# TensorE in source order from the end of the opening, eight slots for each attention unit

## The chip, the cores and the metric

The kernel runs on one core of one Trainium2 chip. The metric is the device time of one execution, in microseconds (us), as the median of several runs. A traced execution of the kernel is read beside it: it has a span, from the first to the last instruction, and a device time of its own.

## The reference

Sliding-window attention with ALiBi biases is followed by a SwiGLU block. There are 8 batches, 8 heads, 576 positions and 64 columns for each head; a query sees itself and the 127 positions before it. The attention output, 4608 tokens by 512 columns, goes through gate and value products to 1536 columns and back to 512. Cut to what matters:

```python
rel = pos[:, None] - pos[None, :]
mask = (rel >= 0) & (rel < 128)
scores = np.where(mask, scale * q @ k.T + slope_h * -abs(rel), -1e9)
attn = softmax(scores)                     # along the keys
x = (attn @ v) -> (4608, 512)
g, val = x @ w_gate, x @ w_val             # (4608, 1536)
out = (g * sigmoid(g) * val) @ w_out       # (4608, 512)
```

## The kernel before

**Attention.** Two batches make a group of 1152 tokens, cut into nine tiles of 128 (eight whole ones, and one that holds the last 64 positions of both batches). There are four groups, so 36 ranks (token tiles) and 36 attention units, numbered i = 0 to 35. A unit's work is in four steps:

- `scores(i)` gives a list of steps: the products of keys and queries on TensorE (tile `ps`, or `psc` for the units at a batch's end), their exponentials on ACT (`ex`, `exc`), and the masks' products on DVE. Unit 9s + p reads k rank 9s + p and q ranks 9s + p and 9s + p + 1.
- `weighted(i)` multiplies with the values (tile `av`) on TensorE and divides by the sums on DVE (tile `x`).
- `x_transposed(i)` brings `x` into the layout of the FFN (tile `xT`): through TensorE (tile `px`) and a copy by ACT for units up to 23, by DMA transposes on SP from 24 on.
- `load(r)` fetches k, q and v of rank r by GpSimd's (POOL's) DMAs, which cast to fp16; `transpose(n)` brings k and q into the layout for scores: on TensorE (tile `pt`) for ranks up to 10, by DMA transposes on SP from rank 11 on. The natural tiles `kn` and `qn` have five buffers each, the transposed ones 12 and 9, the values 12.

**FFN.** Nine blocks of 512 tokens. `gate_val(n, m)` computes 128 columns of gate and value (tiles `pg` and `pv`, four matmuls of 512 columns each), with a tanh on ACT (`tt`) and two products on DVE (`uu`, `hT`). The projection to 512 columns is `project` for block 0 (tile `po`, twelve matmuls of 512 columns for each 128 tokens) and a scheme of seven products on halves, `strassen`, for later blocks. From block 6 on gate and value use seven products too. Block n needs the units whose tokens it holds; `ready` lists how many.

**The order.** `everything` runs the opening, `first_tiles`, written out by hand (units 0 to 3 and the first products of block 0), and then the generator `ffn`, which yields the size of each step it has emitted (1 for a gate or value product, 0.75 for a part of a projection). After each step a target says how many slots of the generator `attention` should have been emitted, and as many are drawn. A slot is what stands between two yields: a step of `scores`, a `weighted`, and so on. `ready` and `blk` are a floor below the target.

What the source says isn't the order on the engines everywhere. Under `tc.manual_schedule` the named engines keep the source's order; elsewhere a scheduler orders the instructions by a simulation of its own. Before, TensorE, DVE and ACT are by hand up to step `ALONE` = 8; then all of them are scheduled; from step `FIXED_FROM` = 60 on TensorE keeps the source's order again. POOL's loads are by hand throughout. SP's queue (transposes and output stores) is scheduled.

In the part of the code that changes, `LATE` = 13 parts two forms of a unit: before it `weighted(i)` follows all of `scores(i + 1)`; from it on `weighted(i)` stands after the third step of `scores(i + 1)`, and `x_transposed` is put off by one unit.

Of the kernel before, what the change touches and what calls it, by code (L numbers as in the profile page):

```python
# [19 lines left out]
X_DMA_FROM = 24  # L20
MASKS_AT = 18.0
ALONE = 8
# [6 lines left out]
FIRST = 4  # L29
LEAD = 6  # L30
PRE = 0
SEVEN_FROM = 6
SILU_AT = 7
SECOND = 5.5
RATE = 54.0
FIXED_FROM = 60
LATE = 13


def slot(h):  # L40

    return 4 * (h // 4) + 2 * (h % 2) + (h % 4) // 2
# [9 lines left out]
def kernel(  # L52
# [95 lines left out]
    def busy(n):  # L148

        t_ = ps_f.tile([P, 512], FP32, name="nil", tag="po", bufs=1)  # L150
        for _ in range(n):
            nc.tensor.matmul(t_, idle[:, 0:P], idle, start=True, stop=True)
# [12 lines left out]
    last = len(units) - 1  # L165
# [28 lines left out]
    def load(rank):  # L194
        load_qk(rank)
        load_v(rank)
# [34 lines left out]
    need = [18 * s + n for s in range(NSUP) for n in (3, 5, 7, 8, 11, 13, 15, 18 if s else 16, 18)]  # L231
# [11 lines left out]
    def scores(i):  # L243

        s, p = units[i]
        def combined(n):
            return scores_128(s, (3, 7, 8)[n], 8, (s, "c", n), msk[n])

        def together(one, two):
            return [one[0] + two[0]] + one[1:] + two[1:]  # L250

        if p == 8:
            first = combined(0) if s == 0 else []
            return first + together(combined(1), combined(2))
        if p == 7 and s == 0:
            return scores_128(s, p, p, (s, p), reg[:, :, 0:P])
        if p == 7:
            return together(scores_128(s, p, p, (s, p), reg[:, :, 0:P]), combined(0))
        if p == 3:
            return scores_128(s, p, p, (s, p), reg[:, :, 0:P], i < FIRST)  # L260
        ks = (9 * s + p) % NK
        banks = []
        early_tile = i < FIRST
        e = epool.tile([P, H, 256], FP16, name="ex", tag="ex", bufs=4)
        ex[(s, p)] = e

        def products():
            for q4 in range(2):
                two = [ps_a.tile([P, 2, 256], FP32, name="ps", tag="a") for _ in range(2)]
                banks.append(two)  # L270
                for par in range(2 if early_tile else 0):
                    o = 4 * q4 + 2 * par
                    nc.tensor.matmul(two[par], idm, bias[:, o:o + 2, :], start=True, stop=False)
                for j in range(2):
                    pair = 2 * q4 + j
                    for par in range(2):
                        rows = slice(64 * par, 64 * par + 64)
                        nc.tensor.matmul(two[par][:, j, :], kT[rows, ks, pair, :],  # L278
                                         qT[rows, p:p + 2, pair, :], start=(j == 0 and not early_tile),
                                         stop=(j == 1))  # L280

        def act(q4, par):
            o = 4 * q4 + 2 * par
            nc.scalar.activation(e[:, o:o + 2, :], banks[q4][par], AF.Exp, scale=scale)  # L284

        def mul(q4):
            if early_tile:
                return
            o = slice(4 * q4, 4 * q4 + 4)
            nc.vector.tensor_mul(e[:, o, :], e[:, o, :], reg[:, o, :])  # L290

        return [[products], [lambda: act(0, 0)], [lambda: act(0, 1), lambda: mul(0)],
                [lambda: act(1, 0)], [lambda: act(1, 1), lambda: mul(1)]]
# [31 lines left out]
    def weighted(i):  # L325

        s, p = units[i]
        x = xpool.tile([P, H, D], FP16, name="x", tag="x")
        xs[i] = x
        for half in range(2):  # L330
            pool, tag = (ps_f, "gv") if i < FIRST else (ps_a, "a")
            av = pool.tile([P, 4, D + 1], FP32, name="av", tag=tag)
            todo = []
            for j in range(4):
                h = 4 * half + j
                if p == 8:
                    for n, kt in enumerate((3, 7, 8)):
                        todo.append((j, ex[(s, "c", n)][:, slot(h), :], va[9 * s + kt][:, h, :]))
                else:
                    if p not in (0, 4):  # L340
                        todo.append((j, ex[(s, p - 1)][:, slot(h), 128:256],
                                     va[9 * s + p - 1][:, h, :]))
                    todo.append((j, ex[(s, p)][:, slot(h), 0:128], va[9 * s + p][:, h, :]))
            for n, (j, w, val) in enumerate(todo):
                nc.tensor.matmul(av[:, j, :], w, val, start=(n == 0), stop=(n == len(todo) - 1))  # L345
            rec = xpool.tile([P, 4, 1], FP32, name="rec", tag="rec", bufs=4)
            nc.vector.reciprocal(rec, av[:, :, D:D + 1])
            nc.vector.tensor_mul(x[:, 4 * half:4 * half + 4, :], av[:, :, 0:D],  # L348
                                 rec.broadcast_to([P, 4, D]))
# [429 lines left out]
    def loads_to(r):  # L779
        nonlocal loaded  # L780
        while loaded <= min(r, NR - 1):
            load(loaded)
            loaded += 1

    def transposes_to(n):
        nonlocal done_t
        while done_t < n:
            transpose(done_t)
            done_t += 1

    def ahead(i):

        n = need[min(i + 4, last)]
        while done_t < n and order[done_t][1] < loaded and order[done_t][1] >= QK_DMA_FROM:
            transposes_to(done_t + 1)

    def run(steps):
        for fs in steps:
            for f in fs:
                f()  # L800
            yield
# [34 lines left out]

    def attention():

        waiting = []
        transposes_to(need[FIRST])  # L840
        for _ in run(scores(FIRST)):
            yield FIRST
        for i in range(FIRST, last + 1):
            late = i >= LATE
            if i < last:
                transposes_to(need[i + 1])
                for n, _ in enumerate(run(scores(i + 1))):
                    yield i - len(waiting)
                    if n == 2 and late:
                        weighted(i)  # L850
                        yield i - len(waiting)
            if not late or i == last:
                weighted(i)
                yield i
            loads_to(i + 7)
            ahead(i)
            yield i - len(waiting)
            if late and i < X_DMA_FROM:
                if waiting:
                    x_transposed(waiting.pop(0))  # L860
                waiting.append(i)
                yield i
                yield i
                continue
            while waiting:
                x_transposed(waiting.pop(0))
            x_transposed(i)
            yield i
            yield i + 1

    def load_w(c0, c1):
        for src, dst in ((wg2, wg_sb), (wv2, wv_sb)):
# [62 lines left out]

    def everything():
        nonlocal done
        base = 0
        busy(WARM)
        with tc.manual_schedule(engines=ENGINES[MANUAL]):  # L940
            first_tiles()
            done = FIRST
            steps = progress(ffn())
            while (at := next(steps)) < ALONE:
                if at == 2.0:
                    nc.scalar.copy(idm2, idm)
                if at in (1.0, 3.0, 4.0):
                    later_masks(2 * (1, 3, 4).index(at) + 2, 2)
        fixed = ExitStack()
        for step in steps:  # L950
            if step >= FIXED_FROM and fixed is not None:
                fixed.enter_context(tc.manual_schedule(engines=ENGINES["pe"]))
                fixed, held = None, fixed
            if step == MASKS_AT:
                make_masks()

            b1 = 24 + 3 * PRE

            lead = LEAD if done < X_DMA_FROM - 2 else LEAD + 4
            blk = (0 if step + LEAD < b1 else 1 if step + LEAD < 60  # L960
                   else min(NBLK - 1, 2 + int((step + lead - 60) // 34.5)))
            if step < b1:

                target = base + 1.25 * max(0, step - ALONE) + 1.5 * max(0, step - 16)
            elif step < 60:
                target = base + 32 + SECOND * 8 * (step - b1) / (60 - b1)
            else:
                target = 84 + (step - 57) * RATE / 34.5
            while (n_att < target or done < ready[blk]) and att_step():
                pass  # L970
        held.close()

    everything()
    queue.close()

# [29 lines left out]
```

## Time and profile before

| | us |
|---|---|
| median of 3 runs (345.45, 346.0, 348.52) | 346.0 |
| profiled execution, its own time | 347.1 |
| its span | 345.3 |
| TensorE (PE) busy | 329.6 (95%) |
| DVE busy | 277.8 (80%) |
| ACT busy | 207.6 (60%) |
| POOL busy | 109.6 (32%) |

The profiled execution is one run of the program with the hardware profiler on. Busy times are unions of an engine's instructions; an engine can be idle because it waits for data, for a free buffer, or because it has nothing to do. A line of a timeline reads: start, length, engine, source line, operation, tile written, tile read, shapes, count, and in brackets how long the engine sat idle before it and what ended that. `PEld` is the loading of weights, which runs beside the matmuls; `POOLq` and `SPq` are DMA issues. DMA load lines show only the issue; the time to landing is a separate figure. Line numbers are those of the kernel before.

### The profile page before, as it was taken

Reading aid. Unit: us, or ns where it says so; the run is one execution under the profiler, and the core shown is the slowest. Engines: PE = TensorE matmul, PEld = TensorE weight load, DVE = VectorE, ACT = ScalarE, POOL = GpSimd, SP = SyncE. Lnnn points to the kernel's source line nnn. Section 1 sums busy time; section 2 is a strip of 40 time slices with the busy share of each in tenths; the row PEclk is TensorE's granted clock in tenths of the full one; section 3 lists DMA queues with packets and bytes.
Section 4 is the critical chain, followed back from the end, with each engine's and each line's share of the span. In section 5 each row is a group of like instructions: output and inputs, shape, how many; then the busy total and the mean of one; then the engine's idle time right before and its main releaser. Section 6 shows DMA issues by size and latency. Waiting matters only on the chain.

```text
span 345.3 us, 7777 instructions
## 1 busy us (share of the span) xinstructions
PE 329.6 (95%) x2983; PEld 218.6 (63%) x2983; DVE 277.8 (80%) x652; ACT 207.6 (60%) x412; POOL 109.6 (32%) x136
## 2 busy tenths in 40 slices
PE   7999987999999999999999999999999999999995
PEld 4484444444456655565565565566788878888884
DVE  6578884999888769998899999999855875775683
ACT  3758675555675666666565646563467676776640
POOL 8967690748665166825008000000000000000000
PEclk9999999999999999999999999999999999999999
DMA  9999999999999999999959904021101101011014
GB/s 152 170 180 175 158 165 154 96 119 157 137 174 138 154 177 161 168 164 135 205 115 103 173 18 93 15 63 47 63 2 61 61 1 64 2 62 63 0 70 116
DMA packets 160037, 37.37 MB, mean 108 GB/s; under 512 B 147328, under 2 KB 155648, under 8 KB 160000
## 3 DMA queue, kind: packets, MB, share of 16 engines
q0 software_dynamic: 118336, 18.62, 85.3%
q1 hardware_dynamic: 40976, 17.64, 27.0%
q10 hardware_dynamic: 688, 0.62, 0.6%
q8 instruction: 23, 0.38, 0.5%
q14 instruction: 14, 0.11, 0.1%
HBM read 37.91 MB, written 9.44 MB: 137 GB/s over the span
## 4 chain that ended last, share of the span: by engine, by line
PE 66%; DVE 17%; DMA 7%; ACT 4%; issue 3%; POOL 2%; SPq 0%; DVEq 0%; ACTq 0%; POOLq 0%
PE po L532 14%; PE pv L397 12%; PE pg L397 12%; PE gX L623 8%; PE gY L623 4%; PE av L345 3%; DMA wo_sb<-in_moe_w_out_dram 3%; DVE uu L416 3%; DMA va<-in_v_dram 3%; PE p L532 2%; DVE hT L427 2%; PE ps L278 2%; PE gZ L623 2%; PE po L451 2%; DVE x L348 2%
## 5 line engine op out<-in xcount | busy, mean ns | idle before, releaser
L397 PE MATMUL pv<-xT,wv_sb 128*128 128x512 f16 (+2 forms) x320 | 76.5, 358 | 0.6 <-DVE uu L416 0.3
L397 PE MATMUL pg<-xT,wg_sb 128*128 128x512 f16 (+2 forms) x320 | 75.8, 358 | 0.3 <-DVE xT L373 0.2
L415 ACT ACTIVATE tt<-pg 128x512 f16<-128x512 f32 (+2 forms) x70 | 41.3, 590 | 50.5 <-PE pg L397 49.5
L284 ACT ACTIVATE ex<-ps 128x512 f16<-128x512 f32 x96 | 50.0, 606 | 11.6 <-PE ps L278 11.6
L416 DVE SCALAR_TENSOR_TENSOR uu<-tt,pg 128x512 f16<-128x512 f16 (+2 forms) x69 | 45.9, 666 | 10.4 <-ACT tt L415 10.2
L427 DVE TENSOR_TENSOR hT<-uu,pv 128x512 f16<-128x512 f16 (+2 forms) x70 | 46.6, 666 | 3.3 <-PE pv L397 1.6
L185 POOL DMA_DIRECT2D va<-in_v_dram x40 | 34.3, 867 | 37.3 <-PE av L345 31.7
L397 PEld LDWEIGHTS <-wg_sb 128*128 128x128 f16 x320 | 28.2, 98 | 24.4 <-issue 2.2
L397 PEld LDWEIGHTS <-wv_sb 128*128 128x128 f16 x320 | 28.3, 98 | 24.1 <-issue 3.0
L532 PEld LDWEIGHTS <-hT 128*128 128x128 f16 x384 | 36.8, 98 | 10.4 <-issue 1.1
L191 POOL DMA_DIRECT2D kn<-in_k_dram x39 | 33.3, 858 | 24.9 <-DMA kT<-kn 13.4
L191 POOL DMA_DIRECT2D qn<-in_q_dram x39 | 33.4, 863 | 13.9 <-DMA va<-in_v_dram 8.0
L532 PEld LDWEIGHTS <-S 128*128 128x128 f16 x288 | 27.6, 98 | 10.7 <-issue 2.5
L290 DVE TENSOR_TENSOR ex<-ex,m_reg 128x1024 f16<-128x1024 f16 x42 | 28.7, 687 | 3.2 <-ACT ex L284 3.1
L348 DVE TENSOR_TENSOR x<-av,rec 128x256 f16<-128x256 f32 x72 | 28.5, 419 | 0.4
L532 PE MATMUL po<-T,S 128*128 128x256 f16 x192 | 26.5, 273 | 0.5 <-DVE S L487 0.5
L532 PE MATMUL po<-T,hT 128*128 128x256 f16 x192 | 26.0, 273 | 0.0
L317 ACT ACTIVATE exc<-psc 128x512 f16<-128x512 f32 x40 | 21.3, 608 | 4.1 <-PE psc L313 4.1
L675 DVE TENSOR_TENSOR hT<-s,v 128x512 f16<-128x512 f16 x18 | 7.6, 423 | 18.5 <-ACT s L674 18.5
L345 PEld LDWEIGHTS <-ex 128*128 128x128 f16 x384 | 17.4, 97 | 4.6 <-issue 1.2
L345 PE MATMUL av<-va,ex 128*128 128x65 f16 x384 | 19.3, 193 | 0.7 <-ACT ex L284 0.7
L278 PE MATMUL ps<-qT,kT 64*128 64x256 f16 x192 | 16.6, 272 | 0.4 <-DVE qT L223 0.2
(134 smaller groups left out, 536.6 us busy)
## 6 DMA issues: line engine op xcount, KB each, us to landing
out_dram<-osb SPq DMA_DIRECT2D x32, 256.0 KB, 2.5
va<-in_v_dram POOLq DMA_DIRECT2D x32, 128.0 KB, 9.0
qn<-in_q_dram POOLq DMA_DIRECT2D x31, 128.0 KB, 7.9
kn<-in_k_dram POOLq DMA_DIRECT2D x31, 128.0 KB, 8.3
wg_sb<-in_moe_w_gate_dram POOLq DMA_DIRECT2D x6, 256.0 KB, 7.7
wv_sb<-in_moe_w_val_dram POOLq DMA_DIRECT2D x6, 256.0 KB, 8.3
wo_sb<-in_moe_w_out_dram POOLq DMA_DIRECT2D x2, 768.0 KB, 9.6
kn<-in_k_dram POOLq DMA_DIRECT2D x8, 64.0 KB, 6.9
```

What stands on the lines that cost most here:

```text
L185: nc.gpsimd.dma_start(va[rank][p0:p1, :, 0:D], src)
L191: nc.gpsimd.dma_start(t_[p0:p1], src)
L284: nc.scalar.activation(e[:, o:o + 2, :], banks[q4][par], AF.Exp, scale=scale)
L290: nc.vector.tensor_mul(e[:, o, :], e[:, o, :], reg[:, o, :])
L345: nc.tensor.matmul(av[:, j, :], w, val, start=(n == 0), stop=(n == len(todo) - 1))
L348: nc.vector.tensor_mul(x[:, 4 * half:4 * half + 4, :], av[:, :, 0:D], rec.broadcast_to([P, 4, D]))
L397: nc.tensor.matmul(ps[:, c0:c1], w[:, kb, ms], xT[n][:, kb, c0:c1], start=(kb == 0 and c0 == 0), stop=(kb == NKB - 1 and c1 == 512), skip_ ...
L415: nc.scalar.activation(tt, pg[:, c0:c1], AF.Tanh, scale=0.5)
L416: nc.vector.scalar_tensor_tensor(out=uu, in0=tt, scalar=one if (n, m) == PIN else 1.0, in1=pg[:, c0:c1], op0=ALU.add, op1=ALU.mult)
L427: nc.vector.tensor_mul(hT[n][:, m, c0:c1], acted[(n, m)][1][:, c0:c1], pv[:, c0:c1])
L532: nc.tensor.matmul(dst, a[:, m, cols], b[:, m, :], start=(start and m == 0), stop=(m == HM - 1), skip_group_check=True)
L623: nc.tensor.matmul(dst[:, i, :], w[:, kb, c0 + i * P:c0 + (i + 1) * P], a[:, kb, :], start=(start and i == 0 and kb == 0), stop=(i == 1 an ...
```

## The change

Three things are replaced.

- `FIXED_FROM` goes from 60 to 9: TensorE keeps the source's order from the end of the opening on. DVE and ACT are scheduled as before.
- `attention` emits eight slots for each unit, whatever its kind: the steps of `scores(i + 1)` in slots 0 on, `weighted(i)` in slot 3, the transposes on TensorE or SP that unit i + 2 needs in slot 5, the loads of rank i + 7 in slot 6, `x_transposed(i)` and the transposes ahead in slot 7.
- The target of slots is no longer computed from `SECOND` and `RATE`, but read off a line through the nine points of `PACE`.

```diff
-SECOND = 5.5
-RATE = 54.0
-FIXED_FROM = 60
-LATE = 13
+PACE = ((9, 0), (10, 1), (12, 2), (14.5, 7), (15, 8), (23.5, 39), (54, 79), (94.5, 127), (187, 263))
+FIXED_FROM = 9
...
     def attention():
 
-        waiting = []
         transposes_to(need[FIRST])
+        yield FIRST
         for _ in run(scores(FIRST)):
             yield FIRST
+        transposes_to(need[FIRST + 1])
+        yield FIRST
         for i in range(FIRST, last + 1):
-            late = i >= LATE
-            if i < last:
-                transposes_to(need[i + 1])
-                for n, _ in enumerate(run(scores(i + 1))):
-                    yield i - len(waiting)
-                    if n == 2 and late:
-                        weighted(i)
-                        yield i - len(waiting)
-            if not late or i == last:
-                weighted(i)
-                yield i
-            loads_to(i + 7)
-            ahead(i)
-            yield i - len(waiting)
-            if late and i < X_DMA_FROM:
-                if waiting:
-                    x_transposed(waiting.pop(0))
-                waiting.append(i)
-                yield i
-                yield i
-                continue
-            while waiting:
-                x_transposed(waiting.pop(0))
-            x_transposed(i)
-            yield i
-            yield i + 1
+            todo = list(scores(i + 1)) if i < last else []
+            for slot in range(8):
+                if slot == 3:
+                    weighted(i)
+                if slot == 5 and i + 2 <= last:
+                    transposes_to(need[i + 2])
+                if slot == 6:
+                    loads_to(i + 7)
+                if slot == 7:
+                    x_transposed(i)
+                    ahead(i)
+                for fs in todo[slot:slot + 1]:
+                    for f in fs:
+                        f()
+                yield i + (slot == 7)
...
-            b1 = 24 + 3 * PRE
-
             lead = LEAD if done < X_DMA_FROM - 2 else LEAD + 4
-            blk = (0 if step + LEAD < b1 else 1 if step + LEAD < 60
+            blk = (0 if step < 24 else 1 if step + LEAD < 60
                    else min(NBLK - 1, 2 + int((step + lead - 60) // 34.5)))
-            if step < b1:
-
-                target = base + 1.25 * max(0, step - ALONE) + 1.5 * max(0, step - 16)
-            elif step < 60:
-                target = base + 32 + SECOND * 8 * (step - b1) / (60 - b1)
-            else:
-                target = 84 + (step - 57) * RATE / 34.5
+            target = np.interp(step, *zip(*PACE))
```

## The prediction

> **What bounds the kernel now.** I read the page first, then the busy time by stretch.
>
> ```profile
> span 345.3 us, 7777 instructions
> ...
> PE 329.6 (95%) x2983; PEld 218.6 (63%) x2983; DVE 277.8 (80%) x652; ACT 207.6 (60%) x412; POOL 109.6 (32%) x136
> ...
> PE   7999987999999999999999999999999999999995
> ...
> PEclk9999999999999999999999999999999999999999
> DMA  9999999999999999999959904021101101011014
> ```
>
> TensorE is busy 95% of the span at full clock, so it is the bound. The 16 DMA engines are also full for the first 200 us; that matters here. By stretch (us; first number after the colon pair is the length, then busy us):
>
> ```profile
> core 0: us, PE busy (x) PEld busy (x) DVE busy (x) ACT busy (x) POOL busy (x), PEclk, DMA share, GB/s
> 26.00:40.00 14.00, 13.41 (x92) 6.46 (x91) 11.73 (x21) 10.84 (x21) 10.47 (x15) 1.00 1.94 175
> 40.00:60.00 20.00, 17.03 (x178) 9.25 (x177) 13.37 (x33) 13.09 (x25) 9.75 (x12) 1.00 1.75 158
> 60.00:76.00 16.00, 15.90 (x108) 7.11 (x107) 15.19 (x29) 9.02 (x17) 8.76 (x10) 1.00 1.88 104
> 76.00:100.00 24.00, 23.09 (x194) 11.40 (x192) 21.70 (x55) 14.54 (x28) 17.91 (x22) 1.00 2.15 154
> ```
>
> TensorE lacks 0.6 us in 26-40, 3.0 in 40-60, 0.1 in 60-76 and 0.9 in 76-100: 4.6 us in all in the part whose order the change rewrites. That is about the most it can win outright. Next, the timeline of TensorE, with the largest single wait and the first scores products of units 10 and 11:
>
> ```profile
> 56.29 0.59 PE L451 MATMUL po<-wo_sb,hT 128*128 128x512 f16 x2 [1.91 <-DMA wo_sb<-in_moe_w_out_dram]
> ...
> 73.56 0.61 PE L278 MATMUL ps<-qT,kT 64*128 64x256 f16 x8
> ...
> 79.87 0.61 PE L278 MATMUL ps<-qT,kT 64*128 64x256 f16 x8
> ```
>
> The 1.91 us wait is project(0) asking for w_out before it has landed. The product at 73.56 is scores(10), the one at 79.87 is scores(11). What can they wait for? The timelines of POOL (loads) and of SP (DMA transposes):
>
> ```profile
> 43.72 1.76 POOL L191 DMA_DIRECT2D qn<-in_q_dram  x2
> ...
> 49.72 0.88 POOL L191 DMA_DIRECT2D kn<-in_k_dram  x1 [0.80 <-DMA wo_sb<-in_moe_w_out_dram]
> 50.59 0.89 POOL L191 DMA_DIRECT2D qn<-in_q_dram  x1
> ...
> 62.88 0.88 POOL L191 DMA_DIRECT2D kn<-in_k_dram  x1 [10.52 <-DMA kT<-kn]
> ```
>
> ```profile
> 59.79 1.30 SPq L239 DMA_TRANSPOSE kT<-kn  x1
> 61.20 1.20 SPq L239 DMA_TRANSPOSE qT<-qn  x1
> 66.18 1.19 SPq L239 DMA_TRANSPOSE kT<-kn  x1
> 67.92 1.24 SPq L239 DMA_TRANSPOSE qT<-qn  x1
> ```
>
> and, for the last of these four transposes (issue 67.92, the query tile of rank 12), its time from issue to landing, and the load that waits for it:
>
> ```profile
> DMA to landing us min/median/max: 8.1/8.1/8.1
> ...
> 76.54 0.87 POOL L191 DMA_DIRECT2D qn<-in_q_dram  x1 [3.56 <-DMA qT<-qn]
> ```
>
> To be seen: POOL stops for 10.52 us, because the load of k rank 12 reuses the buffer that the transpose of k rank 11 reads. So there is a chain that no engine order shortens: k rank 11 lands just before 59.79; its transpose lands just before 62.88; q rank 12 is loaded (landed just before 67.92), transposed, and is there at 67.92 + 8.1 = 76.0. The load at 76.54, released by that landing, agrees. scores(11) reads q ranks 11 and 12, so it cannot run before 76.1. Today it runs at 79.87: 3.8 us of slack. scores(10) needs q rank 11 alone, issued 61.20; the trace gives 2.4 us to landing for it, so 63.6 against 73.56, 9.9 us of slack.
>
> [...] a transpose takes 2.4 us when POOL is stopped, 8.1 us when six loads have been issued since POOL resumed. [...] seven 512-column matmuls in 3.17 us, about 0.43 us each, where later ones start every 0.215. No later idle stretch is longer than 1.91 us.
>
> ```profile
> 1.19 3.17 PE L152 MATMUL nil<-kT 128*128 128x512 f16 x7 [1.19 <-DVE kT L116]
> ```
>
> **The change, part by part.** Amount of work is unchanged: 2983 matmuls, the same operations on DVE and ACT, and the loads on POOL and the transposes on SP stand in the same order. What moves is where the attention stands among the FFN products on TensorE. A wide product (four 512-column matmuls) takes 0.86 us (0.215 each).
>
> *Attention goes forward.* I counted the matmuls ahead of scores(11) from the end of the opening (25.26 us, the same in both). Attention is the same in both: 40 score matmuls of 256 columns, 32 of 128, 88 weighted ones, 80 transposes. FFN is not: 72 gate + 68 value + 24 projection matmuls before, 56 + 56 + 8 after. So 44 matmuls of 0.215 us, 9.5 us, now stand behind scores(11) instead of ahead. For scores(10) the difference is again 44 (9.5 us), for scores(9) 32 (6.9 us), for scores(13) 6.2, for scores(14) 4.4, for scores(15) 2.2, and from scores(16) on both orders agree within 1 us to the end.
>
> *Which waits end last.* From 25.26 us, with the durations of the trace:
> - the transposes of ranks 9 and 10 on TensorE come after 21.5 us of work, some 1 us for the first pv (which frees its PSUM bank by DVE at 27.2 in both) and 1.0 for row-group switches (0.2 each at five score groups, as the gaps at 63.06 show): 48.9-49.5. Their loads, issued 42.84 to 44.6 with 7.2 us to landing, are there at 50.1 to 51.8. Wait about 2.5 us; TensorE is past them at 52.1.
> - scores(9) stands directly behind the transpose of x(7), whose PSUM bank ACT must copy out (0.58 us): about 0.6.
> - scores(10), 8.5 us of work later: ready 60.6, q rank 11 there at 63.6: wait 3.1.
> - scores(11), 6.1 us of work later and 0.3 of switches: ready 70.1, q rank 12 there at 76.0: wait 5.9.
>
> Only the last of these decides, since it ends at 76.1 whatever came before, as long as TensorE arrives earlier (margin 5.9). The 1.91 us wait for w_out goes, because project(0) now starts some 12 us of work later, but that too is inside this sum. After scores(11) the new order has 9.5 us left to do that the old one had done at 79.87. So it lags by 9.5 - 3.8 = **5.7 us**. Queued behind the waiting product on TensorE: a projection, then gate and value products; ACT and DVE run dry behind them.
>
> *Can the lag be made good?* TensorE is full in both, so only by losing fewer waits. scores(9) and scores(13) are no longer cut into pieces; of these only scores(13) lies after 76 us: -0.4. The waits for ACT's ex at 97.14 and 97.62 (0.46 + 0.20) may go: -0.6. Against that scores(13) stands directly behind x(11)'s transpose and waits for ACT's copy as scores(9) does: +0.7. I take -0.3; bounds -2 (all of the 0.9 idle in 76-100 and as much again later, from a DVE that has caught up) and +1.5.
>
> *The clock.* [...] Nothing lost at the low end; at the high end 3.8 us at half clock, as at the start (1.19 to about 5), costs 1.9. I take 0.7.
>
> *The rest at nothing.* SP: output stores of project(0) now stand behind nine pairs of transposes instead of five, so they leave near 100 us instead of 83; there are eight osb buffers and four are used until the second projected block, past 100 us, which hides it; without that cover ACT's copy-out would wait up to those 17 us. POOL's loads wait for landings, not for TensorE, in this stretch, so an earlier slot for loads_to brings none forward.
>
> Sum: 5.7 - 0.3 + 0.7 = 6.1. Profiled execution 347.1 (span 345.3 and 1.8 around it) gives 353.2; the median of the runs shown, 346.0, is 1.1 lower, so 352.1.
>
> **Rivals.**
> - *Cold clock twice.* The 5.9 us wait lowers the clock, and the slots behind it, with DVE and ACT run dry, leave a second stretch at half rate: 346.0 + 5.7 + 2 x 1.9 = 355.5. For: [...] one of 3.1 stands just ahead of it. Against: TensorE has FFN products queued that wait for nothing but weights. 0.15.
> - *Transpose lands earlier.* With different timing of POOL's bursts the transpose of q rank 12 takes no longer than that of k rank 12 just before it (issued 66.18, and a load that waits for it starts at 72.10, so at most 5.9 us; 5.4 to the landing itself): there at 73.3, lag 3.0, 349.0. For: 2.4 us is possible. Against: the loads ahead of it are released by landings alone, hence the same. 0.15.
> - *The other side: no wait at scores(11).* If q rank 12 were there by 70.1, nothing is lost, and the clean order keeps the 4.6 us of idle time of 26-100: 341.4. It decides from a landing before 70.1; q rank 12 itself arrives at 67.9 for its transpose, so this takes one of 2.2 us, below the fastest seen. 0.06.
> - The forecast: 0.64, its own range 350 to 354.
>
> **How the numbers follow.** This kernel's measurement tells about 1% (3.5 us) from no change. Below 342.5: 0.06. Within 1%: the early landing, 0.15. Slower: forecast and cold clock, 0.79. For 8 in 10 I take 347 to 356.
>
> **What would show it.** In the changed profile: TensorE's largest wait is before the first scores product of unit 11, released by DMA qT<-qn, 5 to 6 us, ending near 76; a smaller one of about 3 us before unit 10's, and one of 2 to 3 near 50 for kn or qn; no wait for w_out; the ninth of TensorE's 40 digits (69.1 to 77.7 us) falls to 3 or 4; DVE and ACT idle there too; the lag against before stays 5 to 7 us from 100 us on. Wrong if that transpose lands before 72, if TensorE gets to scores(11) after 74, or if the lag at 100 us is not the lag at the end.

## The result, and the profile after

| | median us | ratio to before, 95% interval |
|---|---|---|
| before, beside the runs of after | 347.26 | |
| after | 356.72 | 1.0273 [1.0207, 1.0339] |

The change makes the kernel slower by 9.5 us. The prediction had the sign and one of the two places; it said 352.1 with a range to 356.0, so the size was 4.6 us short. The profiled execution of after took 357.18 us, 10.1 more than that of before. The page of after:

```profile
span 355.4 us, 7776 instructions
...
PE 332.5 (94%) x2983; PEld 221.6 (62%) x2983; DVE 279.6 (79%) x652; ACT 207.9 (58%) x412; POOL 109.6 (31%) x136
...
PE   7988798959999999999999799999999999999995
...
PEclk9999989989999999999999999999999999999999
```

TensorE's work is the same 2983 matmuls. Against before, TensorE's row has lost in three places: slices 3 to 5 (18-44 us), slice 9 (71-80 us, the 5) and slice 23 (195-204 us, the 7). PEclk falls to 8 in slices 6 and 9: twice in this execution the granted clock was half, for 3.41 us each time. Such a stretch of 3.41 us is called a window below; at half rate it loses 1.7 us of full-clock work where TensorE is busy throughout. The same four stretches as in the prediction:

```profile
core 0: us, PE busy (x) PEld busy (x) DVE busy (x) ACT busy (x) POOL busy (x), PEclk, DMA share, GB/s
26.00:40.00 14.00, 11.87 (x89) 6.08 (x87) 10.65 (x18) 10.65 (x20) 10.75 (x15) 1.00 1.94 175
40.00:60.00 20.00, 17.18 (x180) 9.94 (x178) 15.56 (x37) 14.55 (x28) 9.55 (x11) 0.91 1.75 158
60.00:76.00 16.00, 11.74 (x95) 5.79 (x92) 14.08 (x30) 6.67 (x13) 8.76 (x10) 1.00 1.73 104
76.00:100.00 24.00, 23.44 (x172) 11.75 (x173) 18.56 (x41) 12.79 (x24) 19.11 (x24) 0.93 2.17 147
```

40-60 and 76-100 have a mean clock of 0.91 and 0.93, and 60-76 has 11.7 us of busy TensorE where before had 15.9. The timeline of TensorE there, the first score products of units 10 and 11 and the gate product behind the latter:

```profile
65.03 0.61 PE L276 MATMUL ps<-qT,kT 64*128 64x256 f16 x8
...
76.32 0.61 PE L276 MATMUL ps<-qT,kT 64*128 64x256 f16 x8 [4.06 <-DMA qT<-qn]
...
78.08 1.91 PE L395 MATMUL pg<-xT,wg_sb 128*128 128x512 f16 x4
```

scores(10) waits for nothing. scores(11) waits 4.06 us for the query tile of rank 12; TensorE runs no other matmul in that time, and the gate product behind it runs at half clock (four 512-column matmuls in 1.91 us). The transposes on SP, the load on POOL that the second landing releases, and the transpose's own time:

```profile
66.13 1.19 SPq L237 DMA_TRANSPOSE kT<-kn  x1
67.75 1.25 SPq L237 DMA_TRANSPOSE qT<-qn  x1
```

```profile
76.71 0.87 POOL L189 DMA_DIRECT2D qn<-in_q_dram  x1 [1.56 <-DMA qT<-qn]
```

```profile
DMA to landing us min/median/max: 8.4/8.4/8.4
```

So the chain of landings is what the prediction drew, to 0.2 us: issued at 67.75, 8.4 us to landing, 76.2. What was not in it shows from 100 us on. To compare executions I counted TensorE's work in us at full clock, by the spacing of the matmuls' starts in the traces (0.2155 for a 512-column matmul, 0.109 for 256, 0.055 for 128, 0.0305 for 65, half of that for products on half the rows, which start in pairs, such as those at 63.062 and 63.065 us of before) and read from each trace when the same amount is done; the difference is the lag.

| TensorE work done, us | 50 | 56 | 78 | 98 | 105 | 240 | 309 |
|---|---|---|---|---|---|---|---|
| before, at us | 66.5 | 72.9 | 98.2 | 118.9 | 126.9 | 268.8 | 339.8 |
| after, at us | 68.9 | 81.1 | 104.3 | 125.4 | 133.4 | 279.2 | 350.2 |
| lag | 2.4 | 8.2 | 6.1 | 6.5 | 6.5 | 10.4 | 10.4 |

(At 50 us of work the lag is 1.9 to 2.4, since a short wait lies just there.) At 78 us of work, which is about 100 us of time, the lag is the 6.1 of the prediction's sum. It grows by 3.9 us between 105 and 240 us of work, a stretch that the prediction priced at nothing. The waits of TensorE between 105 and 240 us of time (columns: total, times, longest), first of before, then of after:

```profile
PE po L532 <- DVE osb L536: 1.5, 2, 0.8
PE p L532 <- ACT ex L284: 0.7, 1, 0.7
PE po L532 <- DVE S L487: 0.5, 1, 0.5
PE psc L313 <- DVE osb L536: 0.2, 1, 0.2
```

```profile
PE po L530 <- DVE osb L534: 3.3, 5, 1.9
PE psc L311 <- DVE osb L534: 0.7, 1, 0.7
PE psc L311 <- ACT xT L373: 0.6, 1, 0.6
PE ps L276 <- ACT xT L373: 0.5, 2, 0.2
PE ps L276 <- DVE osb L534: 0.3, 1, 0.3
```

Before loses 1.7 us to the vector engine's (DVE's) copies of a PSUM bank, `osb`, after 4.3 us; and 1.1 us is new, score products that wait for ACT's copy `xT`.

### The profile page after: what moved, and what is told of

It reads as the page before. It is cut to its first block, busy times and chain, and to the rows that moved or that the text cites. A ratio compares the mean times of both kernels' runs of the same rounds, so it can differ in the third digit from the quotient of the medians.

```text
span 355.4 us, 7776 instructions
## 1 busy us (share of the span) xinstructions
PE 332.5 (94%) x2983; PEld 221.6 (62%) x2983; DVE 279.6 (79%) x652; ACT 207.9 (58%) x412; POOL 109.6 (31%) x136
## 4 chain that ended last, share of the span: by engine, by line
PE 65%; DVE 22%; ACT 5%; DMA 3%; issue 3%; ACTq 0%; DVEq 0%
PE po L530 13%; PE pv L395 12%; PE pg L395 12%; PE gX L621 7%; DVE uu L414 4%; PE gY L621 4%; PE av L343 4%; DVE hT L425 3%; PE po L449 3%; PE ps L276 3%; DVE ex L288 2%; DMA qT<-qn 2%; DVE x L346 2%; PE gZ L621 2%; PE p L530 2%
## 5 line engine op out<-in xcount | busy, mean ns | idle before, releaser
L395 PE MATMUL pv<-xT,wv_sb 128*128 128x512 f16 (+2 forms) x320 | 76.2, 361 | 1.7 <-DVE uu L414 1.4
L395 PE MATMUL pg<-xT,wg_sb 128*128 128x512 f16 (+2 forms) x320 | 76.7, 363 | 0.3 <-DVE xT L371 0.2
```

Of the source, the lines that this page charges most:

```text
L395: nc.tensor.matmul(ps[:, c0:c1], w[:, kb, ms], xT[n][:, kb, c0:c1], start=(kb == 0 and c0 == 0), stop=(kb == NKB - 1 and c1 == 512), skip_ ...
```

## The experiments

All ratios are to before on the same chip; medians of different runs can come from different chips. Waits, lags and growth are read from one profiled execution of each kernel. "Growth" is the time from 105 to 240 us of TensorE work in the trace: 141.9 in before, 145.8 in after. The theory after the first comparison was: about 6 us from the chain of landings with the cold clock behind it, about 4 us from the eight-slot form of the late units. Rivals: one cause that shows twice; a slower pace rather than the form; the order alone.

**e4_nat6: one more buffer for the natural k and q tiles.** The load of k rank 12 then need not wait for the transpose of k rank 11.

```diff
-    nat = ctx.enter_context(tc.tile_pool(name="nat", bufs=5))
+    nat = ctx.enter_context(tc.tile_pool(name="nat", bufs=6))
...
-    opool = ctx.enter_context(tc.tile_pool(name="op", bufs=8))
+    opool = ctx.enter_context(tc.tile_pool(name="op", bufs=7))
```

> The changed kernel with six buffers for kn and for qn instead of five (and seven for osb instead of eight, to make room): the load of k rank 12 no longer waits for the transpose of k rank 11. Theory (a chain of landings through the buffers sets the wait before unit 11): k and q of rank 12 land near 62, the transpose of q rank 12 by 68, no wait there and no cold clock behind it; 350 to 352 us. Rival (DMA is full anyhow and the transpose lands as late as before): wait of 3 to 4 us remains, 356 to 357.

350.77 us, 1.0142 [1.0095, 1.0188]: 6 us better than after. POOL's load, TensorE's score product of unit 11, and the clock over the whole span:

```profile
51.47 0.88 POOL L189 DMA_DIRECT2D kn<-in_k_dram  x1 [0.17 <-PE psc L311]
```

```profile
71.47 0.61 PE L276 MATMUL ps<-qT,kT 64*128 64x256 f16 x8
```

```profile
PEclk9999999999999999999999999999999999999999
```

The load of k rank 12 is issued at 51.47 instead of 62.63, the wait before unit 11 is gone, and no half clock is left in this execution. (Of the other three, two took the same time to 0.2 us at a mean clock of 1.000; one took 352.99 us at 0.995, which is what one window makes: 1.7 of 351 us.) The lag is 0.0 at 105 us of work and 3.8 at 240: the growth (145.8) is untouched. About 0.7 us of the gain isn't the landing's: the window at 43 us that after lost doesn't occur here, ahead of the load that the buffer brings forward.

**e2_late_old: units from 13 on in their old form and at their old rate**, the rest as in after; the second loop has the late branch of before as its body.

```diff
+LATE = 13
+RATE = 54.0
...
-        for i in range(FIRST, last + 1):
+        for i in range(FIRST, LATE):
             todo = list(scores(i + 1)) if i < last else []
...
+        waiting = []
+        for i in range(LATE, last + 1):
+            if i < last:
+                transposes_to(need[i + 1])
+                for n, _ in enumerate(run(scores(i + 1))):
...
-            target = np.interp(step, *zip(*PACE))
+            target = np.interp(step, *zip(*PACE)) if step < 54 else 80 + (step - 57) * RATE / 34.5
```

> The changed kernel, but from unit 13 on the attention has the old form (weighted after the third step of scores, x_transposed put off by one unit, the old rate of slots from step 54 on); units 4 to 12 as changed. Theory (landing, clock and late slots): the wait before unit 11 stays at 4 us and the lag is 6 us at 110 us, as in the changed kernel, but it no longer grows to 10 behind that; 352 to 354 us. Rival (the later growth follows from the early lag): 356 to 357 as in the changed kernel.

353.53 us, 1.0202 [1.0171, 1.0232]. The wait before unit 11 stays (3.5 us), the growth is 142.4: the late form, with its rate, costs 3.4 us in this comparison.

**f1_six_old_late: both at once.**

> After, with six load buffers in place of five (as in e4) and with units 13 on in their old form and rate (as in e2). Theory: the change's loss is two separate terms, about 6 us from the chain of landings at units 8 to 12 with the cold clock behind it, and about 4 us from the eight-slot form of the late units. With both taken away the time is that of before: 346 to 348.5, a lag on before of within 1 us at 100 us that stays flat to the end. Rival (the two overlap, part of what e4 won was only room that the late slots then used): 349 to 351, with a lag that grows after 105 us.

346.71 us, 1.0006 [0.9986, 1.0026]: as before. Growth 142.0, lag -0.2 at 105 and 0 at the end. The two edits together take away all of the loss. **f2_before_six** asks whether the buffer is a gain of its own:

> Before, with six load buffers in place of five and nothing else of the change. Theory: before keeps the transpose of each load far enough behind its landing, so the sixth buffer saves only its short waits: 345.5 to 347.5, the same as before. Rival (the sixth buffer is a gain of its own, so that e4 measured the buffer and not the change's chain): 342 to 345.

346.28 us, 1.0012 [0.9988, 1.0037]: it isn't. In before the wait that it removes was not on the path.

**e3_warm: sixteen filler products ahead of scores(11)**, 3.6 us of useless work so that the clock stays up.

```diff
+                for _ in range(16 if i == 11 and q4 == 0 else 0):
+                    nc.tensor.matmul(two[0].rearrange("p a b -> p (a b)"), wg_sb[:, 0, 0:P],
+                                     wg_sb[:, 0, 0:512], start=True, stop=True)
```

> The changed kernel with 16 matmuls of 512 columns on weights put ahead of the first scores product of unit 11, into the same PSUM bank, which the first true product then starts anew: 3.5 us of work in the 4 us in which TensorE waits for q rank 12. Theory: the clock doesn't fall at 77.4 us, and the run is 1.7 us (half of 3.4) shorter than the changed kernel, 355. Rival (the half clock lies beside other work that is late anyhow, DVE and ACT having run dry): no shorter, 356.7, or longer by up to 1 us where the fillers end after the landing.

354.88 us, 1.0241 [1.021, 1.0273], 1.8 us better than after. No half clock behind unit 11 (the gate product takes 1.03 us from 76.34, against 1.91 in after); the query tile landed at 74.34 in this run, during the fillers, and the score product starts at 74.92 without a wait. The total alone doesn't price the clock: that start is 1.4 us earlier than in after, because the tile landed earlier, and a window at half clock at 198.1, which after doesn't have, took 1.7 us back. The stretch behind the wait does: from the start of scores(11) to 63 us of work after took 12.00 us and e3 10.35. So the cold clock is worth the 1.7 us that one window of 3.41 us at half rate takes.

**e1_pace: units 9 to 13 held back by 5 to 10 us of TensorE work, past the landing, and made up for afterwards.**

```diff
-PACE = (... (23.5, 39), (54, 79), (94.5, 127), ...)
+PACE = (... (23.5, 39), (35, 39), (48, 56), (60, 84), (94.5, 127), ...)
```

> The changed kernel with other points of PACE between steps 23.5 and 94.5, so that the scores of units 9 to 13 stand 4 to 10 us of TensorE work later (those of unit 11 after 63.4 us of work, as in the kernel before, instead of 53.1); the eight slots stay. Theory (landing, clock and late slots): the wait for the transpose of q rank 12 and the cold clock behind it go, the loss of 4.2 us that the late units' slots cost from 105 to 240 us stays; 350 to 353 us against 347 before. Rival (the early lag itself disturbs the later waits, through DVE's and ACT's order): both go, 346 to 348. Rival (source order on TensorE costs everywhere): 355 or more.

A miss of the theory: 359.27 us, 1.0357 [1.0323, 1.039]. There is no wait before unit 11, and the lag at 56 us of work is 2.1. But the slots held back came in a bunch, and TensorE waited for the vector engine between them (waits of 84-110 us), until the clock fell for two windows (94.3-101.1 us):

```profile
PE px L369 <- DVE x L346: 3.0, 5, 0.7
```

```profile
PEclk9999989999789999999999999999999999999999
```

The lag is 8.2 at 98, the growth 145.9. The total lies where the last rival put it, but the trace shows no loss everywhere: the loss is the bunch. Here moving the unit past the landing did not pay, because the catching up waited for the vector engine.

**f4_in_order_alone: before, with only the fixed order from step 9.**

```diff
-FIXED_FROM = 60
+FIXED_FROM = 9
```

> Before, with TensorE taken out of the scheduler's hands from step 9 instead of step 60 on, with the old forms and the old targets of attention. Theory: the order alone exposes short waits between 25 and 60 us, 2 to 4 us together and with them possibly half a clock window (1.7 us): 348 to 352, and no growth of the lag after 100 us. Rival (the scheduler's reordering was worth nothing): 346.5 to 347.5. Other rival (the order alone makes the whole loss): 355 to 357.

A miss of all three: 369.23 us, 1.0641 [1.0588, 1.0695], all of it lost before 105 us of work (lag 22.2) and none after. The page, then a stretch of TensorE's timeline:

```profile
PE   7999668988959999999999999999999999999995
...
PEclk9999955999987999999999999999999999999999
```

```profile
57.46 0.40 PE L371 MATMUL px<-idm,x 128*128 128x128 f16 x2 [0.75 <-DVE x L348]
58.61 0.39 PE L371 MATMUL px<-idm,x 128*128 128x128 f16 x2 [0.75 <-DVE x L348]
58.80 1.49 PE L397 MATMUL pg<-xT,wg_sb 128*128 128x512 f16 x3
```

In the old form `x_transposed(i)` follows `weighted(i)` at once. In source order the `px` products wait for the division by the vector engine, 0.75 us at a time in these lines and 10.6 us in 14 waits from 25 to 125 us. Among such short waits the clock was at half for 17.1 us, into a stretch of wide products that wait for nothing (58.80: three in 1.49 us), and for two more windows at 108.3 us. The seven windows make up to 11.9 of the 22 us. So the scheduler had been worth some 22 us on the old form, and it is the eight slots with their pace that make a fixed order bearable.

**g1_slots_scheduled: after, with the fixed order from step 60 only.**

> After, with TensorE's fixed order beginning at step 60 as in before, so that only the slots and their pace remain of the change. The score products of unit 11 stand at the same amount of TensorE work (53.0) as in after. Theory: the fixed order itself costs little once the forms are cut into slots; the waits at the landing for unit 11 and the late slots stay: 353 to 356, the lag at 50 units of TensorE work 0 to 1.5 instead of 2.4, then up to 6 or 7 behind unit 11, then growing by about 4 to the end. Rival (the order is the cause and the scheduler would have found the way around the wait): 349 to 351.

352.68 us, 1.0157 [1.0093, 1.0221], slightly below the theory's range. The early waits go (TensorE is 2.2 us ahead of before at 46 us of work), and so it comes to unit 10 before its landing:

```profile
64.55 0.63 PE L276 MATMUL ps<-qT,kT 64*128 64x256 f16 x8 [2.93 <-DMA qT<-qn]
```

Behind it the clock fell for one window (PEclk is 8 in the slice from 61 to 70 us); the lag is 1.0 at 105, and growth is 145.8. The late loss does not depend on who orders the early part. The early loss does: the wait at unit 11, which the theory kept, is gone. The load of k rank 12 goes out 11 us earlier than in after, with the same five buffers:

```profile
51.70 0.90 POOL L189 DMA_DIRECT2D kn<-in_k_dram  x1
```

It waits for no transpose here, and the query tile of rank 12 is transposed at 65.87 instead of 76.18. So 5.5 of the 6.5 us at 105 are there only with the fixed order and the five buffers together. Why this load finds a free buffer in one order and not in the other, no run takes apart.

**g4_scheduled_six_old_late: g1 with six buffers and the old late form.**

> After with six load buffers, units 13 on in their old form and rate, and the fixed order from step 60 on: of the change only the slots and paces of units 4 to 12 remain. Theory: the early in-order waits (3 us of lag at 34 units of TensorE work in f1, made up by 80) go, and nothing else is late: 345 to 346.5, the same as before or up to 0.4% faster. Rival: 346.5 to 348, the same as f1.

A miss: 351.07 us, 1.0101 [1.0046, 1.0156]. Growth 142.0 as expected, but a 6.81 us wait at unit 10 (timelines of TensorE, POOL and SP):

```profile
68.06 1.04 PE L278 MATMUL ps<-qT,kT 64*128 64x256 f16 x8 [6.81 <-DMA qT<-qn]
```

```profile
57.96 0.87 POOL L191 DMA_DIRECT2D kn<-in_k_dram  x1 [0.20 <-issue]
59.08 0.88 POOL L191 DMA_DIRECT2D qn<-in_q_dram  x1 [0.24 <-issue]
```

```profile
59.36 1.31 SPq L239 DMA_TRANSPOSE kT<-kn  x1
60.78 1.21 SPq L239 DMA_TRANSPOSE qT<-qn  x1
```

With buffers to spare and TensorE ahead, POOL issued two natural loads, k and q of rank 13, at 57.96 and 59.08, ahead of the first transposes. In g1 the former went out at 64.49, after four transposes. The first transpose of a query tile landed at 67.92 here and at 64.41 in g1, for issues at 60.78 and 60.84. That the two loads caused the delay is inferred from these times; no run takes them away alone. So the buffer that saved 6 us in e4 goes with a longer wait than g1's (6.81 us against 2.93) when the engine in front runs earlier.

**The late form: which part of it?** f3 and g2 put `x_transposed(i)` of units 12 to 23 into slot 2 of the next unit; in after it stands in slot 7, right ahead of the next scores. f3 does so in after, g2 in e4.

```diff
...
+                if slot == 2 and waiting:
+                    x_transposed(waiting.pop())
                 if slot == 7:
-                    x_transposed(i)
+                    if 12 <= i < X_DMA_FROM:
+                        waiting.append(i)
+                    else:
+                        x_transposed(i)
                     ahead(i)
...
```

> After, with the transposes of x of units 12 to 23 put into slot 2 of the following unit instead of slot 7 of their own, where they stand right ahead of the next unit's scores. Theory: the late loss has two parts, waits of score products for the copies of these transposes (about 1.8 us in the trace of after) and waits of the output products for bank copies behind the vector engine (about 5 us there, 2.5 in before); only the first goes: 354.5 to 355.5. Rival (the waits move to whatever comes next in order): 356.5 to 357.5, with the same sum of late losses.

> The kernel of e4 (after with six load buffers) with the transposes of x of units 12 to 23 put into slot 2 of the following unit, as in f3. In f3's trace the late loss fell by 1.7 us, but a second half-clock window behind unit 11 took the same amount. Theory: without that window the gain shows: 349.0 (348.3 to 349.7), lag at the end about 2. Rival (the waits move on): 350.5 to 351.2.

f3: 356.17 us, 1.0264 [1.0209, 1.0318]; g2: 349.97 us, 1.0088 [1.0065, 1.0111]. By their totals both look like misses. The growth is 144.0 in both, 1.7 less than in after and e4, as the theory had it; f3 paid as much for a second half-clock window behind unit 11 (74.3-81.1 us, after has 77.4-80.8), g2 came to 105 us of work 0.9 later than e4. g3 gives e4 the old late rate of slots:

```diff
-PACE = (... (54, 79), (94.5, 127), (187, 263))
+PACE = (... (54, 79), (187, 287))
```

> The kernel of e4 (after with six load buffers) with the late pace raised to that of before: points (54, 79) and (187, 287) in place of (54, 79), (94.5, 127), (187, 263), so 1.565 slots a step as 54/34.5 was. Theory (the form costs: transposes of x right ahead of the next scores, output products behind the vector engine's queue): 350 to 352, no better. Rival (the slower pace costs, since attention's vector work then lasts longer beside the output products): 347 to 348.5.

353.43 us, 1.0173 [1.0126, 1.022]: worse, not better. But the old rate of slots doesn't restore the old places (a full-width unit had nine slots, not eight): the score products of units 18 to 33 stand 5 to 11 us of TensorE work earlier than in before, where after and e4 have them up to 2.6 us later. The growth is 145.2, 0.6 less than in e4; the total is worse through 3.2 us lost between 78 and 98 us of work and a window at 43.3 us, ahead of the edit. So a faster pace does not take the late loss away; exactly the old places with eight slots were not tried. h1 (e4) and h2 (f1) leave out the masks' products of the full-width units from 13 on, 0.68 us each on the vector engine.

```diff
-            if early_tile:
+            if early_tile or i >= 13:
                 return
```

> The kernel of e4 (after with six load buffers), without the masks' products on the vector engine (two of 0.68 us a unit) for the full-width units from 13 on; their scores go unmasked. Theory (late loss comes from a full vector engine: bank copies of the output products queue behind its attention work): the lag no longer grows after 105 us, 346 to 348, the waits of output products for osb under 1 us in sum. Rival (the order on TensorE alone makes them wait): 350 to 351.

> The kernel of f1 (six load buffers, late units in the old form), without the same products. Theory: the old form already hides the vector engine's queue apart from some 1.4 us of waits for osb and 0.6 for exc, so it gains 0 to 1.5: 345 to 346.7, and the two forms differ by at most 1.5 us, against 4 with the masks. Rival (the forms differ by TensorE's order): they still differ by about 4 us.

h1: 348.07 us, 1.0029 [1.0009, 1.005], just above its range; h2: 345.14 us, 0.9948 [0.993, 0.9966], in its range. Growth 142.4 and 140.4, the gains 3.4 and 1.6. The eight-slot form gains twice as much from an emptier vector engine, and over this stretch the forms now differ by 2.0 us instead of 3.8. So 1.8 of the 3.8 goes with the vector engine's queue. (By the medians, which include what h2 gains ahead of 105 us, they differ by 2.9 us instead of 4.1.) The waits of h1 at 98-240 us, totals as above, name most of the rest:

```profile
PE po L530 <- DVE osb L534: 1.2, 4, 0.4
PE psc L311 <- ACT xT L373: 0.6, 1, 0.6
PE ps L276 <- ACT xT L373: 0.5, 2, 0.2
PE ps L276 <- DVE osb L534: 0.3, 1, 0.3
```

1.1 us for `xT` is left, the waits that f3 and g2 remove with their gain of 1.7. Counted from the start of one matmul to the start of the next, beyond the cost in the list above, the `xT` waits come to 1.7 us in after and in h1, and those for `osb` to 4.6 in after, 2.2 in before, 1.4 in h1 and 0.4 in h2. Neither theory was right alone: transposes ahead of the scores and the full vector engine both have a part in the late loss, of like size. Each part is read from one execution of each kernel, and no run takes both away at once in the eight-slot form.

How the vector engine does it is seen in after at its longest late wait. Timeline of the vector engine, which is idle at no point of it, and TensorE's product that waits for the second last of these:

```profile
196.60 0.68 DVE L425 TENSOR_TENSOR hT<-uu,pv 128x512 f16<-128x512 f16 x1
197.20 0.69 DVE L288 TENSOR_TENSOR ex<-ex,m_reg 128x1024 f16<-128x1024 f16 x1
197.80 0.68 DVE L414 SCALAR_TENSOR_TENSOR uu<-tt,pg 128x512 f16<-128x512 f16 x1
198.40 0.25 DVE L345 RECIPROCAL rec<-av 128x4 f32<-128x4 f32 x2
198.61 0.76 DVE L346 TENSOR_TENSOR x<-av,rec 128x256 f16<-128x256 f32 x2
199.28 0.41 DVE L534 SCALAR_TENSOR_TENSOR osb<-po,p5s 128x256 f32<-128x256 f32 x1
199.61 0.68 DVE L425 TENSOR_TENSOR hT<-uu,pv 128x512 f16<-128x512 f16 x1
```

```profile
199.75 0.81 PE L530 MATMUL po<-wo_sb,S 128*128 128x256 f16 x6 [1.87 <-DVE osb L534]
```

The copy of the bank (`osb`) stands behind a mask product, two reciprocals and the `x` products of attention, and two products of the FFN. The vector engine was busy 120 of the 135 us from 105 to 240, about 89%; in before 124 of 135. It is as full in both. That in the old form fewer of its long pieces meet just ahead of a bank copy is my reading of this one wait and of the totals above.

No version beat before beyond what is measured; f1 and f2 equal it. h2 is quicker but leaves out work.

## Why the prediction was right and wrong

- *The wait at scores(11).* Right in kind and end (76.3; predicted 76.1), 4.1 us long instead of 5.9: TensorE arrived at 72.26, not 70.1. This error cost nothing, since only the landing sets the end; in e4 the landing comes earlier and the wait is gone. But "there is a chain that no engine order shortens" was wrong: g1, with the scheduler's order and the same five buffers, has that landing at 65.87.
- *The waits before it.* The 2.5 us for the loads of ranks 9 and 10 and the 3.1 us before scores(10) did not occur: TensorE was late enough already, through short waits between 25 and 57 us (1.7 us in two waits for `qT`, 1.0 in two for `exc`, 0.9 for `uu`, 0.7 for `kT`, 0.3 for `x`). The prediction priced the fixed order over that stretch at 2.0 us, for one bank wait and row-group switches (between products on half the rows and on all; two of these, around the score products at 63.06 us of before, took 0.10 and 0.16 us). f4 shows how much such waits can cost, with the half clock that came among them: 22 us.
- *Work shifted, 5.7 us.* Lag at the score product 6.6 by the traces. Right within 1 us. That the waiting product holds back what stands behind it was an estimate; in after no matmul ran from 72.26 to 76.32 us.
- *Made good, -0.3 (bounds -2 to +1.5).* From 8.2 at 56 us of work to 6.1 at 78: -2.1. Too small, outside its bound by 0.1.
- *Clock, +0.7 (bounds 0 to 1.9).* An estimate: the profile of before shows half rate at the start alone, and no fall behind its longest wait after that, 1.91 us. In after one window behind unit 11, 1.7 us; e3's 1.65 behind the wait is of the same size. The value taken was low, the bound right. These two errors cancel: 6.1 to 6.5 at 100 us, sum predicted 6.1. The rival of a cold clock twice named a second stretch behind the wait; the second one in fact came before it, at 43 us, and the lag at 50 us of work, 2.4 at most, holds all that is left of it. That this rival's 355.5 lies nearest to the measurement is luck: it has no late loss either. "TensorE's largest wait, ninth digit 3 or 4": the wait is the largest, the digit is 5.
- *The step that failed: "from scores(16) on both orders agree within 1 us to the end", and so nothing was put down for the late units.* Amounts of TensorE work ahead of each score product were compared, but not what stands directly ahead of it, nor the vector engine's order. (The count itself is off too: in the traces units 20 to 24 stand 1.8 to 2.6 us of work later in after than in before.) The term of the sum should have been 3.9 us: e2 and f1 take it away, f3 and g2 take away 1.7 of it with the transposes of x alone, and 1.8 goes with the vector engine by h1 and h2. The prediction's own sign of failure, "the lag at 100 us is not the lag at the end", is what came: 6.1 to 6.5 and 10.4.
- *Sum.* 6.1 + 3.9 = 10.0, against 10.1 between the two profiled executions and 9.5 between the medians.

## What to carry to other kernels

When a fixed order is rewritten, compare not only how much work stands ahead of each instruction but what stands directly ahead of it and whose result it reads: ten late waits of 0.2 to 1.9 us, 5.4 us in sum where before had 2.9, and small losses around them made 3.9 us here, about the length of the one stall of 4.1 us that the profile shows at once. If a change makes an engine come earlier to a landing, find what sets the landing, and don't take it as fixed when the order of another engine changes: the scheduler's order moved it by 10 us with the same buffers, and a sixth buffer took away 6 us here in one order and left a 6.8 us wait in another. And judge a local edit by the stretch that it touches: the 1.7 us that f3 gained were hidden in its total by an unrelated clock window.

## What the runs showed of the hardware

In after the clock was half from 43.24 to 46.65 us and from 77.37 to 80.79, each 3.41 us. In the traces of after and before the changes of the granted clock lie whole multiples of 3.413 us apart: in after at 5.69, 43.24, 46.65, 77.37, 80.79 and 353.85 us, which is 11, 1, 9, 1 and 80 times that length (the last is at the end of the span), and in before at 5.08 and, behind the last instruction, 346.42, which is 100 times. So windows can be counted on from such a change. The first fall in after came without a long idle stretch: in the 20 us ahead of it no idle gap of TensorE was longer than 1.24 us. The timeline of after:

```profile
40.75 0.62 PE L369 MATMUL px<-idm,x 128*128 128x128 f16 x4 [0.28 <-DVE x L346]
42.60 0.61 PE L276 MATMUL ps<-qT,kT 64*128 64x256 f16 x8 [1.24 <-DVE qT L221]
43.15 1.84 PE L395 MATMUL pv<-xT,wv_sb 128*128 128x512 f16 x4
```

I laid such windows over the nine traces that have a half-clock stretch, and took the work in each, as counted above, as a share of what full clock does in that time. The window just before each of the 23 windows at half clock had 0.00 to 0.36; of the other windows between 20 and 230 us the lowest had 0.38. (Nine of the 23 follow another one at half clock. Those before them were busy for 0.43 to 0.66 of their time, which is 0.21 to 0.33 in work.) In before, where no window between these times is at half clock, the lowest, from 52.87 us on, had 0.39. The same early waits went with a fall in some runs and with none in others. Eleven traces share after's early order. In the five whose windows begin at 43.06 to 43.58 us (after, e1, e2, f3, g3) the clock fell there; in the six whose windows begin at 42.85 and 42.96 (f1, h2) or 44.5 to 44.8 (e3, e4, g2, h1) it didn't. In e3 the window that held most of these early waits had 0.49; its clock fell at 198.1, after a window of 0.36 around the long late wait for `osb`. Behind unit 11 the fall came 5.1 us after the wait began, at 72.26: the window to 73.96 had 0.38, and only the next, with 0.27, was followed by half clock, at 77.37. These shares are counted from one execution of each kernel, and 0.36 and 0.38 lie closer together than the count is sure of: with each matmul counted where it starts, the window ahead of 43.24 us in after and the one to 73.96 both have 0.38. No run changed such a share alone, so none shows where a fall begins.
